# Hashed attention and a gated MLP on one core: weights prepared in DRAM during attention, another order for the first pair, zero matmuls ahead

## The chip, the core and the metric

The kernel runs on one core of a Trainium2 chip. The metric is the device time of one execution in microseconds. A core has five engines that each run their own instructions in program order: TensorE (PE; its weight loads are shown as PEld), VectorE (DVE), ScalarE (ACT), GpSimd (POOL) and SyncE (SP), which here issues nearly all DMAs. Engines wait for each other through semaphores, so a waiting instruction holds up everything behind it on its engine.

## What is computed

Inputs: q, k, v of 4 batches, 8 heads, 768 positions, 64 wide, and the MLP's weights. Everything is float32; the float64 weights w_in and w_out come in as pairs of 32-bit words.

```python
q_bucket = hash of 6 sign bits of q @ proj        # the same for k
scores = where(q_bucket == k_bucket, q @ k.T / 8, -1e9)
attn = softmax(scores);  x = attn @ v             # heads joined: [4, 768, 512]
h = gelu(x @ w_in);  u, v = halves of h           # w_in: [512, 1024]
v_n = layernorm(v) * g_ln
v_s = einsum('ts,bsd->btd', w_sg, v_n) + b_sg     # w_sg: [768, 768]
out = x + (u * v_s) @ w_out                       # w_out: [512, 512]
```

## The kernel before

**Attention** runs over 16 pairs of heads. A pair's q and k come in as one tile each (one buffer: the next pair's load waits until PE has transposed the last one), are transposed on PE (L510), split by ACT and DVE into a high and a low part (L514, L517), and projected for the hash signs (L530, signs on DVE at L533). For each of six query tiles PE forms scores (L550) and DVE takes the row maximum (L555, `mx`); after three of them DVE folds the maxima (L562, `m`) and PE spreads them into a row (L567). Then PE forms the shifted scores of two key tiles at a time (L587, twice 8 matmuls with their halves), ACT takes the exponential (L591, `p`), POOL adds the exponentials up (L604), and after three such groups PE multiplies with v (L616, 24 matmuls). This is called a half here: a pair has two, attention has 32. The sums go to DRAM and back as a reciprocal (L655 to L661), and the half's result xt goes to `xs` in DRAM (L665).

**The MLP** runs over the four batches: `hidden_v` (L780, with gelu and the norm on DVE, ACT and POOL), `hidden_u` (L811), `gate` (L829: all eight PSUM banks are filled tile by tile of w_sg, so that the six tiles are needed one after the other), and `project` (L858).

**Weights.** w_in is taken apart in 16 jobs (`weight_job`, L364 to L388: a load, one POOL multiply, seven DVE steps, one ACT copy), which the planner lets run from the start in DVE's gaps, at the lowest priority. `gate_weights` (L746 to L751) runs after attention: each of the six 128-row tiles of w_sg comes in by four DMAs with pieces of 32 floats (128 bytes), is transposed by DVE, and split by ACT and POOL. `out_weights` takes w_out apart in 16 jobs of half the width (tiles `ow...`, also on L364 to L383) after attention, beside the first gate.

**Order.** The order on each engine is set when the program is built: `Plan` places all steps by costs and priorities (`prio`, two units for a group of attention), with constants such as HID (where `hidden_v` of batch 0 comes in) and WP (priority of the weight jobs). PSUM has eight banks; score tiles take two. In hardware each engine just runs its list.

Of the kernel before, what the change touches and what calls it, by code (L numbers as in the profile page):

```python
# [21 lines left out]
MLP = {"xl": "POOL", "gm": "DVE", "gl": "POOL", "wg": 472.02, "wo": 74.3, "x": 467.58}  # L22
# [3 lines left out]
HID = 275.02  # L26
# [9 lines left out]
class Plan:  # L36
# [76 lines left out]
    def order(self):  # L113
# [13 lines left out]
        free, seq, ready, dma_free, pe, till, lanes = {}, {}, {}, 0.0, {}, {}, []  # L127
# [122 lines left out]
def kernel(  # L250
# [55 lines left out]

    frow = setup.tile([1, 4, P], F32, name="frow")
# [13 lines left out]
    nc.vector.tensor_copy(identr, ident)  # L321
# [9 lines left out]
    msts = [const.tile([P, HT, P], F32R, name=f"m{i}") for i in range(2)]  # L331
    for m in msts:
        nc.vector.memset(m.bitcast(F32), 0.0)
# [8 lines left out]
    wjobs = [(w_in, c, f0, CW, wih, wil, 1.0) for f0 in range(0, FF, CW) for c in range(NC)]  # L342

    def weight_job(plan, tile_of, src, c, f0, CW, th, tl, fac, prio, bank=None, mark=None):
        def part(t):
            return (t() if isinstance(t, Plan.Buf) else t)[:, c, f0:f0 + CW]

        bufs = [(t, (c, f0)) for t in (th, tl) if isinstance(t, Plan.Buf)]
        w = tile_of([P, CW, 2], I32, "w64")
        x, g = tile_of([P, CW], I32, "wx"), tile_of([P, CW], F32, "wg")  # L350
# [570 lines left out]
```

## Time and profile before

| | |
|---|---|
| median of 3 runs | 760.76 us (760.44 to 763.42) |
| the profiled execution, its own time | 760.57 us |
| its span, first to last instruction | 758.7 us |
| PE busy | 731.9 us, 96% of the span |
| DVE / POOL / ACT busy | 557.0 / 466.0 / 375.1 us |
| attention, start to the last product with v | 0 to 446.8 us |
| MLP | 446.8 us to the end |

A busy PE is PE with a matmul in flight. Where PE is busy nearly always, time can only come from its idle stretches, from stretches at the lower clock, and from work that is taken off it. PE's idle before an instruction, with the engine that ended it, is in its timeline and in the list of waits.

### The profile page before, as it was taken

Reading aid. Unit: us, or ns where it says so; the run is one execution under the profiler, and the core shown is the slowest. Engines: PE = TensorE matmul, PEld = TensorE weight load, DVE = VectorE, ACT = ScalarE, POOL = GpSimd, SP = SyncE. Lnnn points to the kernel's source line nnn. Section 1 sums busy time; section 2 is a strip of 40 time slices with the busy share of each in tenths; the row PEclk is TensorE's granted clock in tenths of the full one; section 3 lists DMA queues with packets and bytes.
Section 4 is the critical chain, followed back from the end, with each engine's and each line's share of the span. In section 5 each row is a group of like instructions: output and inputs, shape, how many; then the busy total and the mean of one; then the engine's idle time right before and its main releaser. Section 6 shows DMA issues by size and latency. Waiting matters only on the chain.

```text
span 758.7 us, 14327 instructions
## 1 busy us (share of the span) xinstructions
PE 731.9 (96%) x5348; PEld 594.8 (78%) x5348; DVE 557.0 (73%) x905; ACT 375.1 (49%) x616; POOL 466.0 (61%) x496
## 2 busy tenths in 40 slices
PE   4999999999999999999999999989799999999997
PEld 4686777768787777868686669878798889988996
DVE  6978888988898889887575548669955866447733
ACT  2475565647556664755564456435632236106510
POOL 0478788888868687877767665767753414503230
PEclk9999999999999999999999999999999999999999
DMA  8133444244334423431311125820121552052003
GB/s 184 25 78 78 89 110 118 69 116 123 89 99 106 109 51 96 109 78 50 96 54 33 32 63 111 167 63 21 39 89 56 117 140 69 1 124 44 1 0 111
DMA packets 174597, 60.87 MB, mean 80 GB/s; under 512 B 156736, under 2 KB 167104, under 8 KB 174528
## 3 DMA queue, kind: packets, MB, share of 16 engines
q1 hardware_dynamic: 174080, 59.31, 32.6%
q8 instruction: 42, 0.69, 0.4%
q10 hardware_dynamic: 448, 0.66, 0.3%
q14 instruction: 27, 0.22, 0.1%
HBM read 47.16 MB, written 12.78 MB: 79 GB/s over the span
## 4 chain that ended last, share of the span: by engine, by line
PE 80%; DVE 10%; DMA 5%; issue 2%; ACT 2%; SPq 1%; POOL 0%; DVEq 0%; POOLq 0%; ACTq 0%
PE psb L587 17%; PE psb L616 15%; PE psb L829 11%; PE psb L550 8%; PE psb L858 8%; PE psb L780 6%; PE psb L811 5%; PE psb L530 4%; PE psb L510 3%; PE psb L638 2%; DMA x<-xs 2%; DMA gs<-in_moe_w_sg_dram 1%; DVE mx L555 1%; DMA k<-in_k_dram 1%; PE psb L567 1%
## 5 line engine op out<-in xcount | busy, mean ns | idle before, releaser
L604 POOL TENSOR_TENSOR sum<-sum,p 128x384 f32<-128x384 f32 x256 | 248.8, 1007 | 0.0
L555 DVE TENSOR_REDUCE mx<-psb 128x2 f32<-128x768 f32 x192 | 181.0, 956 | 48.5 <-PE psb L550 41.0
L591 ACT ACTIVATE p<-psb 128x768 f32<-128x768 f32 x192 | 155.3, 814 | 61.5 <-PE psb L587 55.6
L616 PE MATMUL psb<-p,v 128*64 128x385 f32 x768 | 131.2, 491 | 0.0
L604 POOL TENSOR_TENSOR sum<-p,p 128x384 f32<-128x384 f32 x64 | 63.8, 1017 | 73.8 <-ACT p L591 73.8
L616 PEld LDWEIGHTS psb<-p,v 128*64 128x64 f32 x768 | 52.3, 137 | 64.1 <-issue 62.9
L550 PE MATMUL psb<-fk,fq 64*128 64x384 f32 x384 | 68.4, 352 | 1.8 <-DVE fk L533 0.9
L829 PE MATMUL psb<-wgl,zh 128*128 128x384 f32 x192 | 65.4, 340 | 3.7 <-POOL wgl L751 3.7
L587 PE MATMUL psb<-hq,hk 64*128 64x384 f32 x384 | 65.7, 338 | 2.8 <-ACT p L591 1.6
L829 PE MATMUL psb<-wgh,zh 128*128 128x384 f32 x192 | 65.2, 340 | 1.0 <-ACT wgh L750 1.0
L829 PE MATMUL psb<-wgh,zl 128*128 128x384 f32 x192 | 65.1, 339 | 0.0
L587 PE MATMUL psb<-fq,fk 64*128 64x384 f32 x384 | 64.6, 332 | 0.0
L550 PE MATMUL psb<-hk,hq 64*128 64x384 f32 x384 | 64.6, 332 | 0.0
L587 PE MATMUL psb<-lq,hk 64*128 64x384 f32 x384 | 64.5, 332 | 0.0
L587 PE MATMUL psb<-hq,lk 64*128 64x384 f32 x384 | 64.5, 332 | 0.0
L840 POOL TENSOR_TENSOR gs<-gt,gs 128x384 fp32r<-128x384 f32 x32 | 34.1, 1072 | 48.0 <-ACT gs L837 48.0
L858 PE MATMUL psb<-woh,gs 128*128 128x512 f32 x192 | 60.4, 391 | 0.1
L629 ACT COPY un<-psb 128x385 f32<-128x385 f32 x32 | 15.4, 482 | 86.8 <-PE psb L616 86.8
L765 DVE SCALAR_TENSOR_TENSOR h<-h,psb 128x384 f32<-128x384 f32 (+1 forms) x56 | 33.1, 604 | 28.9 <-ACT h L764 28.6
L764 ACT ACTIVATE h<-psb 128x384 f32<-128x384 f32 (+1 forms) x56 | 29.3, 533 | 43.3 <-PE psb L780 39.7
L811 PE MATMUL psb<-xh,wih 128*128 128x384 f32 x128 | 43.6, 341 | 4.1 <-DVE y L769 4.1
L796 POOL TENSOR_TENSOR zl<-y,zh 128x512 fp32r<-128x512 f32 x24 | 32.5, 1353 | 23.6 <-ACT zh L795 23.5
(120 smaller groups left out, 1593.1 us busy)
## 6 DMA issues: line engine op xcount, KB each, us to landing
q<-in_q_dram SPq DMA_DIRECT2D x32, 192.0 KB
k<-in_k_dram SPq DMA_DIRECT2D x32, 192.0 KB
v<-in_v_dram SPq DMA_DIRECT2D x16, 384.0 KB
rs<-r SPq DMA_DIRECT2D x64, 96.0 KB
xs<-xt SPq DMA_DIRECT2D x32, 192.0 KB
x<-xs SPq DMA_DIRECT2D x16, 384.0 KB
rx<-xs SPq DMA_DIRECT2D x96, 64.0 KB
out_dram<-ob SPq DMA_DIRECT2D x24, 256.0 KB
```

The costliest lines, as they stand in the source:

```text
L550: nc.tensor.matmul(sc[kh]()[:, j, :SH], x[0]()[row(j), qs], x[1]()[row(j), kh * SH:(kh + 1) * SH], start=(n == 0), stop=(n == 1))
L555: plan.add(DVE, 0.95, prio, lambda kh=kh: nc.vector.tensor_reduce(mx()[:, i, :, kh], sc[kh]()[:, :, :SH], axis=AX.X, op=ALU.max, negate=Tr ...
L587: nc.tensor.matmul(sc[i]()[:, j, :SH], x()[row(j), ks], y()[row(j), cs], start=(n == 0), stop=(n == 3))
L591: plan.add(ACT, 0.81, prio, lambda i=i: nc.scalar.activation(p[i]()[:, :, :SH], sc[i]()[:, :, :SH], AF.Exp), [sc[i]], [p[i]])
L604: plan.add(POOL, 1.03, prio + 0.6, lambda i=i, j=j, first=first: nc.gpsimd.tensor_add(sums()[:, j], (first or sums)()[:, j, :SH], p[i]()[: ...
L616: nc.tensor.matmul(av()[row(j), :SH + 1], v_()[:, j, kt, :], p[kt]()[:, j, :], start=(kt == 0), stop=(kt == NT - 1))
L765: plan.add(DVE, us + 0.07, prio, lambda: nc.vector.scalar_tensor_tensor(h2()[:, :n], h2()[:, :n], 1.0 / GA, ps()[:, :n], op0=ALU.add, op1= ...
L780: nc.tensor.matmul(ps(), x()[:, ts_], w[:, c, FH:FF], start=(c == 0 and n == 0), stop=(c == NC - 1 and n == 2))
L811: nc.tensor.matmul(ps()[:, :SH], w[:, c, fs], x()[:, cs], start=(c == 0 and n == 0), stop=(c == NC - 1 and n == 2))
L829: nc.tensor.matmul(vp()[:, :SH], z()[:, t, fs], w()[:, t, cs], start=(t == 0 and n == 0), stop=(t == NT - 1 and n == 2))
L840: nc.gpsimd if e == POOL else nc.vector).tensor_sub(gl()[:, cs], gt(), gh()[:, cs].bitcast(F32)),
L858: nc.tensor.matmul(po(), a()[:, ts_], w()[:, f, :], start=(f == 0 and n == 0), stop=(f == NF - 1 and n == 2))
```

## The change

- **Start.** One of the two zeroed tiles `m0` is cleared first; nine matmuls of it with itself (five, then four) are issued ahead of PE's first real work. A few constants move from DVE to POOL (`identr`, half of `pw`). v of the first pair is planned behind its k, g_ln's load behind the first weight job. Weight jobs are planned from the fourth group on, not from the start.
- **w_in** keeps its 16 jobs, each with the same steps, with other priorities (a job every 3.3 groups, then rising).
- **w_out** is taken apart in 8 jobs of full width that follow w_in's in attention. High and low part go to DRAM (`wo_h`, `wo_l`, L382); `out_weights` just loads them (L782).
- **w_sg** is copied DRAM to DRAM in attention, the 128-byte pieces put where the tiles want them (`wgd`, L728, four DMAs in each of pairs 4 to 9); `gate_weights` then loads whole rows (L773). Transposing and splitting stay.
- **Constants** of the planner are other numbers, so the order moves everywhere. EASE is 0, so its branches aren't taken.

```diff
-MLP = {"xl": "POOL", "gm": "DVE", "gl": "POOL", "wg": 472.02, "wo": 74.3, "x": 467.58}
+MLP = {"xl": "POOL", "gm": "DVE", "gl": "POOL", "wg": 463.01, "wo": 6.18, "x": 476.31}
-HID = 275.02
+HID = 282.35
-PREP, SHIFTP, FINP, WSTEP, WP = 5.01, -1.49, 6.21, 37.69, 60
+PREP, SHIFTP, FINP, WSTEP, WP = 4.19, -0.76, 8.79, 37.69, 30
+GPLACE = 4
+EASE = 0
+RATE = 2.45
+WFROM = 7.86
...
+    nc.vector.memset(msts[0].bitcast(F32), 0.0)
...
-    nc.vector.tensor_copy(identr, ident)
+    nc.gpsimd.tensor_copy(identr, ident)
...
+    ojobs = [(w_out, c, f0, CW, None, None, 0.5) for f0 in range(0, DM, CW) for c in range(NF)]
...
+        if th is None:
+            for t, dst, mk in ((hi_, wod[0], wodb[0]), (lo_, wod[1], wodb[1])):
+                plan.add("SP", 0.57, prio, lambda t=t, dst=dst: nc.sync.dma_start(dst[:, c, f0:f0 + CW], t().bitcast(F32)),
+                         wh if t is hi_ else wl, [(mk, (c, f0))], dma=0.4)
...
+    for i in range(5):
+        nc.tensor.matmul(psb[:, 6, :P], msts[0][:, 0].bitcast(F32), msts[0][:, 0].bitcast(F32), start=True, stop=True)
     for i in range(4):
         nc.tensor.transpose(psb[:, 7, i:i + 1], frow[:, i, :], ident[:1, :1])
     nc.vector.tensor_copy(fcol, psb[:, 7, 0:4])
+    for i in range(4):
+        nc.tensor.matmul(psb[:, 6, :P], msts[0][:, 0].bitcast(F32), msts[0][:, 0].bitcast(F32), start=True, stop=True)
...
-        for i, job in enumerate(wjobs):
-            weight_job(plan, w_tile, *job, WSTEP * i + WP, BANKED and ps_one or None, win)
...
+                if c == 1 and GPLACE <= n < GPLACE + NT:
+                    t = n - GPLACE
+                    for h in range(P // Q):
+                        c0 = t * P + h * Q
+                        dma(2 * g + 20, 0.6, lambda eng, t=t, h=h, c0=c0: eng.dma_start(
+                            wgd[t][h * Q:(h + 1) * Q].rearrange("b (f a) -> b f a", a=Q),
+                            w_sg[:, c0:c0 + Q].rearrange("(f b) a -> b f a", b=Q)), [ticks[-1]], [(wgdb, (t, h))])
+                while conv and WFROM + RATE * conv[0][0] <= 2 * g:
+                    at_, job, args = conv.pop(0)
+                    job(plan, w_tile, *args, 2 * g + WP, after=[ticks[-1]])
...
     def gate_weights(prio):
-            for g in range(P // Q):
-                c0 = t * P + g * Q
-                dma(prio + t - 5, 0.6, lambda eng, w=w, g=g, c0=c0: eng.dma_start(
-                    w()[g * Q:(g + 1) * Q].rearrange("b (f a) -> b f a", a=Q),
-                    w_sg[:, c0:c0 + Q].rearrange("(f b) a -> b f a", b=Q)), w=[(w, g)], e=WSG)
+            dma(prio + t - 5, 1.1, lambda eng, w=w, t=t: eng.dma_start(w(), wgd[t]), [wgdb], [w])
...
     def out_weights(prio):
-        CO = 128
-        for f0 in range(0, DM, CO):
-            for c in range(NF):
-                weight_job(plan, lambda sh, dt, tag: tile_of(sh, dt, "o" + tag, 1), w_out, c, f0, CO, woh, wol, 0.5, prio)
+        for c in range(NF):
+            for i, w in enumerate((woh, wol)):
+                dma(prio + c, 0.75, lambda eng, i=i, w=w, c=c: eng.dma_start(w()[:, c, :].bitcast(F32), wod[i][:, c, :]), [wodb[i]], [(w, c)])
```

Three places show what the planner makes of it. The first is DVE at the start, from the first pair's low part of k (lk) to the second pair's. `wy`, `wx`, `wil` are steps of a weight job, `fq` and `fk` the signs, `mx` the maxima. Before:

```order
L517 SCALAR_TENSOR_TENSOR lk_0_279<-psb,hk_0_274 128x768
L373 TENSOR_SCALAR wy_283<-w_0_247 128x256
L533 TENSOR_SCALAR fq_0_291<-psb,fcol 128x768
L374 SCALAR_TENSOR_TENSOR wx_293<-w_0_247,wy_283 128x256
L375 SCALAR_TENSOR_TENSOR wx_293<-wg_281,wx_293 128x256
L377 TENSOR_SCALAR wy_283<-wx_293 128x256
L533 TENSOR_SCALAR fk_0_303<-psb,fcol 128x768
L378 SCALAR_TENSOR_TENSOR wy_283<-w_0_247,wy_283 128x256
L386 TENSOR_TENSOR wx_293<-wx_293,wy_283 128x256
L517 SCALAR_TENSOR_TENSOR lq_0_317<-psb,hq_0_310 128x768
L555 TENSOR_REDUCE mx_93<-psb 128x2 x6
```

The same stretch of DVE now:

```order
L520 SCALAR_TENSOR_TENSOR lk_0_284<-psb,hk_0_282 128x768
L541 TENSOR_SCALAR fq_0_286<-psb,fcol 128x768
L541 TENSOR_SCALAR fk_0_306<-psb,fcol 128x768
L520 SCALAR_TENSOR_TENSOR lq_0_310<-psb,hq_0_300 128x768
L568 TENSOR_REDUCE mx_96<-psb 128x2 x6
L575 TENSOR_REDUCE m_71<-mx_96 128x6
```

The weight steps are gone from there. The second place is DVE in one late half of attention (between the 24th and the 25th `m`). Before:

```order
L663 SCALAR_TENSOR_TENSOR xt_4049<-un_3614,rs_3972 128x384
L533 TENSOR_SCALAR fq_6_4061<-psb,fcol 128x768
L533 TENSOR_SCALAR fk_6_4083<-psb,fcol 128x768
L657 RECIPROCAL sq_4023<-sq_4023 128x6
L373 TENSOR_SCALAR wy_4088<-w_15_3933 128x256
L374 SCALAR_TENSOR_TENSOR wx_4091<-w_15_3933,wy_4088 128x256
L375 SCALAR_TENSOR_TENSOR wx_4091<-wg_3989,wx_4091 128x256
L377 TENSOR_SCALAR wy_4088<-wx_4091 128x256
L378 SCALAR_TENSOR_TENSOR wy_4088<-w_15_3933,wy_4088 128x256
L555 TENSOR_REDUCE mx_93<-psb 128x2 x6
```

The same half of DVE now:

```order
L541 TENSOR_SCALAR fq_6_4089<-psb,fcol 128x768
L673 RECIPROCAL sq_4053<-sq_4053 128x6
L541 TENSOR_SCALAR fk_6_4114<-psb,fcol 128x768
L377 TENSOR_TENSOR wx_3961<-wx_3961,wy_3955 128x256
L371 TENSOR_SCALAR wy_4122<-w_15_4036 128x256
L379 SCALAR_TENSOR_TENSOR wil<-wx_3961,wih 128x256
L372 SCALAR_TENSOR_TENSOR wx_4131<-w_15_4036,wy_4122 128x256
L568 TENSOR_REDUCE mx_96<-psb 128x2
L373 SCALAR_TENSOR_TENSOR wx_4131<-wg_4137,wx_4131 128x256
L375 TENSOR_SCALAR wy_4122<-wx_4131 128x256
L376 SCALAR_TENSOR_TENSOR wy_4122<-w_15_4036,wy_4122 128x256
L377 TENSOR_TENSOR wx_4131<-wx_4131,wy_4122 128x256
```

Five weight steps have become eight; before, the jobs end with the half after this, now they go on to the end of attention. The third place is SP behind attention's last sums (`r`, `rs`), where the tiles `gs` of w_sg are loaded. Before:

```order
L746 DMA gs_5637<-in_moe_w_sg_dram 32x24x32 x4
L665 DMA xs_111<-xt_5680 128x384
L665 DMA xs_111<-xt_5698 128x384
L746 DMA gs_5732<-in_moe_w_sg_dram 32x24x32 x2
L364 DMA ow_0_5749<-in_moe_w_out_dram 128x256
L851 DMA rx_5757<-xs_108 32x16x32 x4
L851 DMA rx_5785<-xs_108 32x16x32 x4
L727 DMA x_5820<-xs_109 128x768
L746 DMA gs_5732<-in_moe_w_sg_dram 32x24x32
```

SP at the same place now:

```order
L773 DMA gs_5774<-wgd 128x768
L677 DMA rs_5788<-r_0_236 64x384 x2
L677 DMA rs_5817<-r_1_238 64x384 x2
L773 DMA gs_5833<-wgd 128x768
L773 DMA gs_5864<-wgd 128x768
L681 DMA xs_111<-xt_5880 128x384
L681 DMA xs_111<-xt_5902 128x384
L773 DMA gs_5923<-wgd 128x768
L782 DMA woh_5952<-wo_h 128x512
```

Tiles four to six now stand ahead of the loads for `project` (rx), with one DMA each.

## Rows read from the trace of the kernel before

**Rows 1.** The page: busy time in us (share of the 758.7) and instructions by engine

```profile
PE 731.9 (96%) x5348; PEld 594.8 (78%) x5348; DVE 557.0 (73%) x905; ACT 375.1 (49%) x616; POOL 466.0 (61%) x496
```

**Rows 2.** PE's timeline, MLP: start, us, line, out<-in, [idle before <-who ended it]

```profile
488.94 0.44 PE L829 MATMUL psb<-wgl,zh 128*128 128x384 f32 x1 [1.46 <-POOL wgl L751]
494.22 0.44 PE L829 MATMUL psb<-wgh,zh 128*128 128x384 f32 x1 [0.99 <-ACT wgh L750]
496.87 0.69 PE L829 MATMUL psb<-wgl,zh 128*128 128x384 f32 x1 [2.21 <-POOL wgl L751]
...
537.58 0.45 PE L811 MATMUL psb<-xh,wih 128*128 128x384 f32 x1 [1.55 <-DVE y L769]
542.52 0.45 PE L811 MATMUL psb<-xh,wih 128*128 128x384 f32 x1 [2.55 <-DVE y L769]
```

**Rows 3.** PE's timeline at the start of the kernel

```profile
4.58 1.51 PE L510 MATMUL psb<-ident,q 128*128 128x128 f32 x6 [2.16 <-DMA q<-in_q_dram]
8.62 1.51 PE L510 MATMUL psb<-ident,k 128*128 128x128 f32 x6 [2.52 <-DMA k<-in_k_dram]
...
10.88 0.52 PE L530 MATMUL psb<-hq,pwh 128*128 128x384 f32 x1
...
12.48 0.33 PE L530 MATMUL psb<-hk,pwl 128*128 128x384 f32 x1
...
14.62 0.85 PE L510 MATMUL psb<-ident,q 128*128 128x128 f32 x6 [1.63 <-DMA q<-in_q_dram]
16.31 0.44 PE L550 MATMUL psb<-fk,fq 64*128 64x384 f32 x2 [0.85 <-DVE fk L533]
```

**Rows 4.** The chain that ended last, its pieces up to 40 us: start, us, what

```profile
14.08 0.34 DVE wx L374
...
25.73 0.43 DVE wx L374
26.16 1.00 DVE fk L533
```

**Rows 5.** SP's timeline at the start: the first pair's q and v, and the next q

```profile
0.74 1.02 SPq L493 DMA_DIRECT2D q<-in_q_dram  x2
...
2.98 4.81 SPq L499 DMA_DIRECT2D v<-in_v_dram  x2
...
9.26 0.95 SPq L493 DMA_DIRECT2D q<-in_q_dram  x2
```

**Rows 6.** PE's timeline in attention: two products with v

```profile
204.67 4.10 PE L616 MATMUL psb<-p,v 128*64 128x385 f32 x24
...
230.80 4.10 PE L616 MATMUL psb<-p,v 128*64 128x385 f32 x24
```

**Rows 7.** Busy time by window, engines in turn; then PEclk, DMA share, GB/s

```profile
45.00:337.00 292.00, 290.35 (x2631) 217.84 (x2632) 255.18 (x340) 172.84 (x263) 233.56 (x241) 1.00 0.38 95
...
494.00:500.00 6.00, 3.57 (x11) 3.32 (x12) 2.86 (x6) 1.61 (x4) 4.25 (x5) 0.72 0.57 122
...
542.50:550.00 7.50, 7.48 (x34) 7.49 (x35) 7.08 (x16) 6.12 (x14) 6.28 (x6) 0.77 0.20 56
```

**Rows 8.** Groups by line, DVE, 45 to 337 us: count | busy, mean ns | idle

```profile
L386 DVE TENSOR_TENSOR wx<-wx,wy 128x256 f32<-128x256 f32 x14 | 11.4, 811 | 0.3
...
L373 DVE TENSOR_SCALAR wy<-w 128x256 int32<-128x256 int32 x13 | 9.4, 726 | 1.6 <-DMA w<-in_moe_w_in_dram 1.5
```

**Rows 9.** DVE's timeline: one weight step beside POOL's sums

```profile
113.36 1.11 DVE L374 SCALAR_TENSOR_TENSOR wx<-w,wy 128x256 int32<-128x256 int32 x1
```

**Rows 10.** DVE's timeline in the MLP: a tile of w_sg, and its wait

```profile
485.08 0.98 DVE L749 STREAM_TRANSPOSE gs<-gs 128x768 f32<-128x768 f32 x1 [2.85 <-DMA gs<-in_moe_w_sg_dram]
```

**Rows 11.** Busy time by window (last half of attention; hidden_v), DVE alone, then PEclk, DMA share, GB/s

```profile
412.46:428.61 16.15, 7.84 (x12) 1.00 0.12 38
...
520.00:545.00 25.00, 23.89 (x56) 0.98 0.09 28
```

**Rows 12.** PE's waits in the whole span: total us, times, longest us

```profile
PE psb L587 <- ACT p L591: 1.6, 4, 0.5
```

More of the change, by code (lines that the diff above doesn't have):

```diff
@@ L330 @@
         nc.vector.memset(t[:, :, :, 2:3], EMPTY)
[L331 to L333 removed]
+    nc.vector.memset(msts[1].bitcast(F32), 0.0)
     fcol = const.tile([P, 4], F32, name="fcol")
@@ L366, in vec @@
         def vec(fn, r, wr, fast=False):
-            plan.add("DVE", 0.16 + CW / (1920.0 if fast and port else 960.0), prio, fn, r, wr, port=port)
-        lo, hi, xf, zi = (lambda: w()[:, :, 0]), (lambda: w()[:, :, 1]), (lambda: x().bitcast(F32)), (lambda: zf().bitcast(I32))
-        plan.add("SP", 0.55, prio - 2, load, [], [w], dma=0.73 * CW / 256)
+            plan.add("DVE", 0.14 + CW / (1920.0 if fast else 960.0), prio, fn, r, wr, port=True)
+        lo, hi, xf, yf, xi = (lambda: w()[:, :, 0]), (lambda: w()[:, :, 1]), (lambda: x().bitcast(F32)), (lambda: y().bitcast(F32)), x
@@ L395 @@
     win = plan.buf("win", 1)
+    wod = [dram.tile([P, NF, DM], F32, name=f"wo_{i}") for i in "hl"]
+    wgd, wgdb = dram.tile([NT, P, S], F32, name="wgd"), plan.buf("wgdb", 1)
+    wodb = [plan.buf(f"wodb{i}", 1) for i in range(2)]
     xd = [[plan.buf(f"xd_{b}_{c}", 1) for c in range(NC)] for b in range(B)]
@@ L521, in parts @@
             plan.add(ACT, 0.81, prio, high, [tp], [hh])
-            plan.add(DVE, 0.95, prio, low, [tp, hh], [lo])
+            if 1 <= st.n <= EASE:
+                ft = st.ft[s]
+                plan.add(ACT, 0.81, prio, lambda: nc.scalar.mul(two(ft).bitcast(F32), tp()[:, :, :SH], fac), [tp], [ft])
+                plan.add(POOL, 1.88, prio, lambda: nc.gpsimd.tensor_sub(lo(), ft().bitcast(F32), hh().bitcast(F32)), [ft, hh], [lo])
+            else:
+                plan.add(DVE, 0.95, prio, low, [tp, hh], [lo])
         def features(st, s, prio):
@@ L536, in features @@
             plan.add(PE, 1.044, prio, project, [hh, lo, ft], [fp])
-            plan.add(DVE, 1.07, prio, sign, [fp], [ft])
+            if 1 <= st.n <= EASE:
+                plan.add(ACT, 0.81, prio, lambda: nc.scalar.copy(two(ft).bitcast(F32), fp()[:, :, :SH]), [fp], [ft])
+                plan.add(POOL, 1.88, prio, lambda: nc.gpsimd.tensor_scalar(
+                    ft(), ft().bitcast(F32), fcol[:, 2 * s:2 * s + 1], fcol[:, 2 * s + 1:2 * s + 2], op0=ALU.is_gt, op1=ALU.mult), [ft], [ft])
+            else:
+                plan.add(DVE, 1.07, prio, sign, [fp], [ft])
         def largest(st, t, prio):
```

64 lines of the change are left out of this document (31 added, 33 removed).

## The prediction, made before the kernel was run

> **What bounds the kernel now.** I read the page's busy times first: PE is busy for 731.9 of 758.7 us [rows 1], so only its 26.8 us of idle time, and stretches at a lower granted clock, are to be had. PE's timeline then says where these are. At the start it waits 2.16 us for q, 2.52 for the first k, 1.63 for the second q and 0.85 for `fk` [rows 3]; smaller waits lie between. In the MLP five waits make 8.8 us: 1.46 + 0.99 + 2.21 = 4.66 for tiles of w_sg inside the first gate, and 1.55 + 2.55 = 4.10 for DVE's `y` in `hidden_v` of batch 1 [rows 2]. In attention PE hardly waits: four waits for ACT, 1.6 us together, are the largest item [rows 12].
>
> The windows add the clock [rows 7]. From 45 to 337 us it is granted in full. From 494 to 500 us the mean is 0.72 and from 542.5 to 550 us 0.77: each time PE had just stood idle, and part of the window ran at the lower of the two levels (1.2 instead of 2.4 GHz). At the start the same shows in single matmuls: 0.52 us, later 0.33 [rows 3], after PE had waited for loads.
>
> The profiled execution took 760.57 us, 1.87 more than its span and 0.2 under the median; the sum is made against 760.57.
>
> **The start.** Before, v (two transfers, 768 KB) is issued ahead of everything but q and k, taking SP until 7.8 us, and the next q follows only at 9.26 [rows 5]. Now v stands behind the next q. Three things follow.
>
> (a) k shares the queues with less. q, issued at 0.74, was there at 4.58, so a k without v beside it should be ready when PE has transposed q, at about 6.1: up to 2.5 us earlier than 8.62 [rows 3, 5]. (b) The next q's transposes (0.85 us, up to 1.5 at the low clock [rows 3]) now stand on PE ahead of k's projections, not behind them. That load can be issued when PE has read the old tile, at about 6; issuing takes 0.95 [rows 5], and landing took 2.8 us for the first q (1.76 to 4.58) and 4.4 for the second (10.21 to 14.62): it arrives at 9.8 to 11.4. With its transposes, k's six projections (1.1 us, 1.9 at the low clock) and `fk` (1.0 [rows 4]), `fk` is done at 12.7 to 15.8. Before, it was done just ahead of 16.31, where the scores begin [rows 3]: 0.5 to 3.5 us are won. (c) The chain that ended last runs through eight weight steps on DVE, the first at 14.08 us, the last at 25.73 ahead of the second pair's `fk`, 2.97 us in all [rows 4]. Three lie ahead of the first `fk`, in (b)'s stretch; the other five, 1.8 us, behind it. The second order piece shows them gone.
>
> Together 2.3 to 5.3, with 3.8 in the middle. The nine zero matmuls lie inside the wait that ends at 4.58: nine of 0.25 us (1.51 / 6 [rows 3]) are 2.3 us, and about 4 us pass there nearly without work on PE, so they cost nothing if `m0` is cleared in time. What they can bring is the clock: six projections at 0.32 us apart, where later ones are 0.17 apart [rows 3], are 0.9 us, most of it beside waits for loads; I count 0.2. The start is worth **−4.0**. If the next q lands late, PE stands there with k's projections behind it, and the first `fk` gains nothing; with half of the later steps covered by something else, −1.0 is the other bound.
>
> **The MLP's first gate.** All eight banks are filled tile by tile, so a late tile stops PE. Tiles come in by pieces of 128 bytes; DVE waited 2.85 us for one [rows 10]. Now whole rows are read and, as the third order piece shows, all six tiles stand ahead of rx. The 4.66 us go, and with them the slow stretch: 6 us at 0.72 are 1.7 us too much, 1.4 after what idle time of it has been counted. The pieces of 128 bytes now move in pairs 4 to 9, where the queues are 0.38 busy [rows 7] and nobody waits for the result; hidden. What is late next is a tile's transpose (0.98 us on DVE [rows 10]) and split on ACT and POOL, which now have all of `hidden_v` of batch 0 ahead of them.
>
> **The MLP's `hidden_v`.** From 520 to 545 us DVE is busy 23.89 of 25 us [rows 11], so DVE is the bound there. Of the 56 steps there 21 belong to w_out; at the mean of 23.89 / 56 = 0.43 us they are 9 us. With w_out ready in DRAM they go, DVE needs 15 of the 25 us, and 4.10 + 7.5 × 0.23 = 4.10 + 1.7 us [rows 2, 7] go too. The eight loads of w_out, 256 KB each, have the whole first gate to land.
>
> Sum of the MLP: −(4.66 + 1.4 + 4.10 + 1.7) = **−11.9**. The other bound is one of the two places keeping its stall: −5.8.
>
> **Attention pays.** Eight more jobs put 56 steps on DVE, 8 on POOL and 8 on ACT, and 24 placements, 16 stores and 8 loads on SP, whose stores wait for ACT and DVE with the next q and k queued behind; q and k have a whole pair's time, so that is hidden. DVE is the question. Two products with v of the same half lie 230.80 − 204.67 = 26.13 us apart, a half is 13.07 [rows 6]. From 45 to 337 us DVE is busy 255.2 us [rows 7], of which 97 weight steps in seven groups (the first and the last are shown [rows 8]) have 72.1 us, 0.743 each. The other 183.1 us over 22.3 halves are 8.2 us a half. 13.07 − 8.2 leaves room for 6.5 steps.
>
> Counted between the `m` of the order now, halves 4 to 20 hold 3 to 6 steps, as before. From the 21st on the counts are 8, 6, 7, 5, 8, 7, 6, 3, 7, 6, 7 and 11 in the last. A half of 8 needs 14.14 us, 1.07 too much: 2.1 for two. A half of 7 is 0.33 over, 1.3 for four, hidden if the maxima run ahead as in the halves with room. The last half took 16.15 us from `m` to `m`, since `hidden_v` already runs in it, and DVE was busy for 7.84 of them [rows 11]; with 11 steps (8.2) and two more of `hidden_v` (1.4, by what its steps take in the MLP) it needs 17.4, 1.3 too much. Between 2.1 and 4.7 I take **+3.5**. Bounds: 0, if `m` has slack everywhere; +10, if a step in the twelve full halves costs 0.85, near the 0.81 group [rows 8] (8.2 + 6.75 × 0.85 = 13.94, 0.87 over, 10.4 for twelve). The waits for ACT [rows 12] stay.
>
> Sum: 760.57 − 4.0 − 11.9 + 3.5 = **748.2 us**.
>
> **Rivals.** *DVE's steps beside POOL (slower).* A weight step next to POOL's sums took 1.11 us [rows 9], half as much again as the mean. If the twelve full halves run at that, each needs 8.2 + 6.75 × 1.11 = 15.7 and is 2.6 us too long: +31, and 760.57 − 15.9 + 31 = **776**. It is as slow as before from 15.9 = 12 × (8.2 + 6.75 s − 13.07), s = 0.92 us per step. For it: the 1.11; against it: 97 steps at a mean of 0.743 in a stretch in which POOL was busy 80% of the time [rows 7]. On this mechanism the Trainium skill ("SBUF — State Buffer", section "SBUF: two separate sides") has a rule that DVE and GpSimd share a port pair as a lock held for a whole instruction. By it alone a step that meets one of POOL's sums waits for its end, as the 1.11 us suggest [rows 9], and the time would be this rival's; by the mean of 0.743 most steps meet none, or POOL waits instead.
>
> *One stall stays.* Clearing the gate's loads or DVE shows the next late thing in the same place, about half of the 11.9: **754**. For it: five waits on three engines in one stretch [rows 2]; against: both causes are removed, not moved.
>
> *The start doesn't gain.* The next q's load is late, −1.0 instead of −4.0: **751**.
>
> *Only moved.* w_out's steps cost in attention what they cost in the MLP: +10 instead of +3.5, **755**; with one of the MLP's stalls left as well it is 760, no change.
>
> **How the numbers follow.** Forecast with its own range 743 to 751: 0.58. One stall left 0.13, no gain at the start 0.10, only moved 0.10, slower by DVE 0.09. A measurement of this kernel can tell about 0.5%, 3.8 us: faster is under 757.0, slower over 764.4. Faster: 0.58 + 0.13 + 0.10 + 0.04 of the moved ones (755 to 760) = 0.85; same: 0.06 of these and 0.02 of the slower case, 0.08; slower 0.07. The range reaches from all bounds at their best, 760.57 − 5.3 − 11.9 = 743.4, with the clock's 0.9 us 742, to 757, which takes in one stall or moved work.
>
> **What will show it.** Right: the scores begin at 11 to 14 us instead of 16.31, no PE wait of over 0.5 us for `wgh`, `wgl` or `y` in the MLP, a full granted clock there, 13.1 to 14.2 us between products with v late in attention, and PE idle of 10 to 13 us in all. Wrong: PE waiting for `m` or for the maxima in the halves from 21 on (DVE), weight steps over 0.9 us there, PE waiting for the second q at the start, or a tile of w_sg or w_out that arrives late because its placement did.

## The result, and the profile after

The changed kernel takes 749.21 us (median of 4 runs, 747.89 to 750.39) against 761.81 us before (4 runs, 760.44 to 763.42): the ratio is 0.983, with a 95% interval of 0.980 to 0.986. The profiled execution took 750.39 us, the slowest of its four, with a span of 748.6; all that follows is read from it and set against the 758.7 us of span before. So between the two profiles the change is 10.1 us, and between the medians 12.6.

The page of the changed kernel: span, then PE's busy time (share of span) and instructions. PE is busy 734.2 us, 2.3 more than before [rows 1], while the span is 10.1 shorter.

```profile
span 748.6 us, 14297 instructions
PE 734.2 (98%) x5366; PEld 593.1 (79%) x5366; DVE 564.2 (75%) x876; ACT 368.9 (49%) x592; POOL 452.8 (60%) x461
```

Busy share says little of where the 10.1 us come from. The starts of the 32 products with v on PE's timeline cut the span in stages (us from the span's start):

| | 1st product | 30th product | last product | end of span |
|---|---|---|---|---|
| before | 33.66 | 413.71 | 442.75 | 758.7 |
| after | 29.91 | 415.98 | 449.19 | 748.6 |

So the start won 3.75 us, the 29 halves behind it lost 6.02 (386.07 instead of 380.05), and from the last product on 16.54 are won. In the last pair 12 more matmuls of `hidden_v` (0.23 us each) now stand between the 30th and the 31st product, 24 where 12 were. Those 2.8 us only changed sides of the cut: of the 4.17 us lost between the 30th and the last product 1.4 are a loss, and the MLP won 13.7.

**The MLP** has lost its waits and its slow stretches. These are the windows of [rows 7] again in the changed kernel: busy time of PE, PEld, DVE, ACT and POOL, then PEclk, DMA share, GB/s.

```profile
494.00:500.00 6.00, 6.00 (x37) 5.97 (x35) 2.75 (x5) 2.41 (x4) 4.63 (x4) 1.00 0.91 205
542.50:550.00 7.50, 7.50 (x44) 7.50 (x43) 6.31 (x13) 6.22 (x12) 3.22 (x4) 1.00 0.00 1
```

Both are full and at the full clock, and no wait of PE of 0.15 us or more is left behind the last product; in [rows 2] there were five.

**The start**, PE's timeline of the changed kernel (start, us, operation, idle before):

```profile
1.32 2.50 PE L427 MATMUL psb<-m 128*128 128x128 f32 x10 [1.32 <-DVE m L311]
3.61 1.91 PE L432 MATMUL psb<-m 128*128 128x128 f32 x8
5.46 0.40 PE L429 MATMUL psb<-ident,frow 1*128 1x1 f32 x4
5.79 0.87 PE L513 MATMUL psb<-ident,q 128*128 128x128 f32 x6
6.50 0.82 PE L513 MATMUL psb<-ident,k 128*128 128x128 f32 x6
...
10.99 0.85 PE L513 MATMUL psb<-ident,q 128*128 128x128 f32 x6 [1.38 <-DMA q<-in_q_dram]
...
14.07 0.45 PE L563 MATMUL psb<-fk,fq 64*128 64x384 f32 x2 [1.17 <-DVE fk L541]
```

k no longer waits (2.52 us in [rows 3]), and the scores begin at 14.07 instead of 16.31. But the nine zero matmuls are 18 instructions on PE, not nine: PE is at them until about 5.46, and q's transposes, at 4.58 before, begin at 5.79.

**Attention** lost 6.0 us without showing them as idle: the waits of 0.15 us or more between the 1st and the 30th product sum to 2.5 us (1.55 before). Late in attention PE is busy 122.19 of 123 us, before 123.00, and yet does less. The window from 280 to 403 us, before and then after, engines as above:

```profile
280.00:403.00 123.00, 123.00 (x1118) 92.76 (x1116) 95.14 (x126) 71.58 (x108) 94.41 (x100) 1.00 0.31 78
```

```profile
280.00:403.00 123.00, 122.19 (x1080) 89.38 (x1077) 111.63 (x158) 71.52 (x111) 95.06 (x101) 1.00 0.38 98
```

DVE has 16.5 us more to do there and is busy 91% of the time. What PE pays is seen in one half, the one from 307.87 to 322.40 (14.53 us, the same half 13.49 before). First DVE, then PE, in the middle of it:

```profile
313.02 0.96 DVE L568 TENSOR_REDUCE mx<-psb 128x2 f32<-128x768 f32 x1 [1.16 <-PE psb L563]
...
315.02 0.42 DVE L373 SCALAR_TENSOR_TENSOR wx<-wg,wx 128x256 f32<-128x256 f32 x1
315.48 0.29 DVE L375 TENSOR_SCALAR wy<-wx 128x256 int32<-128x256 int32 x1
315.80 1.24 DVE L376 SCALAR_TENSOR_TENSOR wy<-w,wy 128x256 f32<-128x256 uint32 x1
316.96 3.54 DVE L568 TENSOR_REDUCE mx<-psb 128x2 f32<-128x768 f32 x4
```

```profile
316.61 0.34 PE L602 MATMUL psb<-fq,fk 64*128 64x384 f32 x2
316.90 0.44 PE L563 MATMUL psb<-fk,fq 64*128 64x384 f32 x2
317.18 0.34 PE L563 MATMUL psb<-hk,hq 64*128 64x384 f32 x2
317.97 0.45 PE L602 MATMUL psb<-hq,hk 64*128 64x384 f32 x2 [0.45 <-DVE mx L568]
```

Three weight steps stand between two maxima, and PE waits for the banks that the maxima hold. Only 0.45 us of it are listed as idle. The matmul at 316.90 starts 0.29 behind the one ahead of it and lasts 0.44 instead of 0.33, and the next starts 0.28 behind it; the distance is 0.17 elsewhere. So some 0.2 us are lost there that count as busy. This half has five matmuls of scores or projections with such a long head (over 0.42 us), the same half before has two. Over the eleven halves from the 19th to the 30th product there are 36 of them, before 16, and these halves lost 5.05 us, of which 0.8 are listed as idle: about 0.2 us for each head more. So here the distance between products must be read, not the idle column. And the half isn't full: ahead of the maximum at 313.02 DVE stands idle for 1.16 us, waiting for PE.

### The profile page after: what moved, and what is told of

Its sections match the earlier page's. It is cut to its first block, busy times and chain, and to the rows that moved or that the text cites. A ratio compares the mean times of both kernels' runs of the same rounds, so it can differ in the third digit from the quotient of the medians.

```text
span 748.6 us, 14297 instructions
## 1 busy us (share of the span) xinstructions
PE 734.2 (98%) x5366; PEld 593.1 (79%) x5366; DVE 564.2 (75%) x876; ACT 368.9 (49%) x592; POOL 452.8 (60%) x461
## 4 chain that ended last, share of the span: by engine, by line
PE 91%; DVE 5%; DMA 2%; issue 1%; ACT 1%; SPq 0%; DVEq 0%; ACTq 0%
PE psb L602 16%; PE psb L632 16%; PE psb L853 13%; PE psb L835 9%; PE psb L563 9%; PE psb L882 9%; PE psb L804 9%; PE psb L538 5%; PE psb L513 3%; DVE mx L568 2%; PE psb L654 2%; PE psb L580 1%; DVE wy L376 1%; DMA w<-in_moe_w_in_dram 1%; DVE wy L375 1%
## 5 line engine op out<-in xcount | busy, mean ns | idle before, releaser
L568 DVE TENSOR_REDUCE mx<-psb 128x2 f32<-128x768 f32 x192 | 178.3, 954 | 26.7 <-PE psb L563 22.2
L620 POOL TENSOR_TENSOR sum<-p,p 128x384 f32<-128x384 f32 x64 | 65.3, 1041 | 84.8 <-ACT p L607 84.7
L563 PE MATMUL psb<-fk,fq 64*128 64x384 f32 x384 | 70.7, 362 | 2.9 <-DVE mx L568 1.6
L814 POOL TENSOR_TENSOR mv<-mv,epsr 128x1 f32<-128x1 f32 x24 | 13.8, 576 | 90.2 <-DVE mv L813 90.2
L856 DVE TENSOR_TENSOR gt<-psb,b_bc 128x384 f32<-128x384 f32 x32 | 17.7, 555 | 49.7 <-PE psb L853 45.9
L563 PEld LDWEIGHTS psb<-fk,fq 64*128 64x128 f32 x384 | 36.3, 184 | 18.6 <-issue 5.6
```

Of the source, the lines that this page charges most:

```text
L563: nc.tensor.matmul(sc[kh]()[:, j, :SH], x[0]()[row(j), qs], x[1]()[row(j), kh * SH:(kh + 1) * SH], start=(n == 0), stop=(n == 1))
L568: plan.add(DVE, 0.95, prio, lambda kh=kh: nc.vector.tensor_reduce(mx()[:, i, :, kh], sc[kh]()[:, :, :SH], axis=AX.X, op=ALU.max, negate=Tr ...
L620: plan.add(POOL, 1.03, prio + 0.6, lambda i=i, j=j, first=first: nc.gpsimd.tensor_add(sums()[:, j], (first or sums)()[:, j, :SH], p[i]()[: ...
```

## The experiments

All change the changed kernel. The stages of each run, as above. The twelve matmuls of `hidden_v` (2.8 us) that changed sides stand ahead of the last product in the changed kernel, in the run with w_sg gathered, with the jobs begun 3 groups earlier, with no or six zero matmuls and with the jobs spread; in the other five they stand behind it, as before, so the column of the last product is 2.8 us lower there.

| run | median, us (runs) | 1st product | 30th | last | span |
|---|---|---|---|---|---|
| changed kernel | 749.21 (4) | 29.91 | 415.98 | 449.19 | 748.6 |
| no w_out steps on DVE | 745.78 (4) | 29.51 | 413.61 | 441.50 | 744.5 |
| w_out in the MLP | 760.40 (10) | 29.73 | 414.18 | 443.24 | 759.1 |
| w_sg gathered in the MLP | 759.86 (10) | 30.06 | 417.35 | 450.40 | 758.7 |
| weight jobs early | 755.81 (7) | 29.04 | 422.16 | 451.24 | 754.0 |
| jobs begun 3 groups earlier | 748.86 (4) | 29.32 | 415.45 | 446.77 | 746.7 |
| no zero matmuls | 746.17 (1) | 28.94 | 413.28 | 445.04 | 744.4 |
| the same, pw on DVE | 750.61 (1) | 30.99 | 415.70 | 447.47 | 748.8 |
| six zero matmuls, pw on DVE | 746.11 (1) | 29.26 | 413.23 | 444.99 | 744.3 |
| the same, timed | 747.33 (5) | 29.44 | 413.55 | 445.35 | 745.7 |
| ... and two buffers for w | 749.68 (4) | 29.46 | 411.62 | 440.70 | 748.0 |
| ... or two for wx and wy | 746.83 (4) | 28.79 | 413.44 | 442.56 | 745.1 |
| ... and two for w, jobs spread | 745.47 (4) | 28.89 | 412.27 | 443.78 | 743.7 |

### Does DVE's work on w_out cost attention its time?

```diff
 def weight_job(plan, tile_of, src, c, f0, CW, th, tl, fac, mark, prio, after=()):
+    if th is None:
+        # load, POOL's multiply into g, one ACT copy into y, stores of y and g
+        return
```

> The changed kernel with the seven DVE steps of each of w_out's eight jobs left out: the load, POOL's multiply, one ACT copy and the two stores to DRAM stay, so that what is stored for w_out is not its value. Measure: from the 19th to the 30th product with v the kernel before took 143.3 us, the changed one 148.4. Theory (DVE's steps between the maxima cost it): the halves in which only w_out's steps ran, the 25th to the 30th, get back to 13.07 (1.8 us), the last half loses its wait for ACT's exponentials (1.4): some 146.5 us for the stretch, 2 to 4 us less in all, 745 to 747. Rival (stores, loads, POOL or the queues cost it): 148 us and 749.

It took 745.78 us, ratio to before 0.980 (0.978 to 0.983), some 3.4 us under the changed kernel. From the 24th to the 30th product it needs 78.44 us, before 78.50, the changed kernel 80.34: the 1.8 us came back as expected. The whole stretch from the 19th product is 147.4, not 146.5, because the five halves from the 19th to the 24th product stay long: 68.97 us, 68.03 in the changed kernel, 64.84 before. There all steps are w_in's, 8, 6, 7, 5 and 8 a half, where before there were 4 or 5. So of attention's 6.0 us 1.8 come from DVE's steps of w_out, which this run shows, and 3.2 lie where only w_in's jobs run, which the new priorities push together; that these jobs are the cause is argued from the place here.

### Could w_out stay in the MLP?

```diff
-    ... (weight_job, 2.7, [w + (None,) for w in ojobs])
-            dma(prio + c, 0.75, lambda eng, ...: eng.dma_start(w()[:, c, :].bitcast(F32), wod[i][:, c, :]), ...)
+            # 16 jobs of 128 columns in out_weights: five DVE steps, three of POOL, two of ACT each
```

> The changed kernel with w_out converted in the MLP beside the first gate, as before (16 jobs of half width, five DVE steps each), w_sg still placed in attention. Theory: attention as in the run without w_out's steps (146.5 us from the 19th to the 30th product), and hidden_v of batch 1 short of DVE again, 4.1 + 1.7 us and some small waits: 749.2 - 3 + 6.3 = 752.5. Rival (the gate's late tiles were the whole stall, and the order now leaves DVE room in the MLP): 746.

With it the planner's constant `wo`, the place of `out_weights`, is back at 74.3. It took 760.40 us, ratio 1.000 (0.998 to 1.002): 8 us more than expected, and against both theories. Attention did as expected (146.9 us). The MLP cost 13.6 us more (315.86 from the last product, with 2.8 us of matmuls on this side, against 299.41), as long as before (315.95). PE's timeline there:

```profile
534.79 0.44 PE L859 MATMUL psb<-xh,wih 128*128 128x384 f32 x1 [2.92 <-DVE y L817]
570.67 0.50 PE L906 MATMUL psb<-woh,gs 128*128 128x512 f32 x1 [2.83 <-DVE y L817]
575.64 0.50 PE L906 MATMUL psb<-woh,gs 128*128 128x512 f32 x1 [1.64 <-ACT woh L804]
576.61 0.80 PE L906 MATMUL psb<-wol,gs 128*128 128x512 f32 x1 [0.47 <-POOL wol L805]
```

The first wait is of the kind in [rows 2]; the others are new. DVE's steps of w_out by tile (min/median/max ns, first and last start), and one place on DVE's timeline, say why:

```profile
L797 DVE TENSOR_SCALAR owy<-ow x16: 219/228/970, 474.0 to 572.6; 128x128 int32<-128x128 int32 x16
```

```profile
530.09 0.23 DVE L797 TENSOR_SCALAR owy<-ow 128x128 int32<-128x128 int32 x1 [1.44 <-DMA ow<-in_moe_w_out_dram]
```

The sixteen jobs share one buffer and so form one chain, with loads that DVE waits for in between (11.3 us in seven waits) and `y` behind them. Its first steps run from 476.3 to 570.2 us before, when the gate waits for its tiles, and from 474.0 to 572.6 here, where the gate waits for none: it is no faster. `project` of batch 0, which needs its results, begins at 564 us (577 before) and still waits for them at 575. In the changed kernel w_out is there early, and `project` begins at 503. So the conversion, not the gate's tiles, set the end of this stretch: taking away the tiles' stall alone only moved the wait to the chain's end. w_out's move is worth 13.6 us in the MLP on top of w_sg's, not the 5.8 that I had counted.

### Could w_sg be gathered by the gate itself?

```diff
-                if c == 1 and GPLACE <= n < GPLACE + NT: ... # four placements
-            dma(prio + t - 5, 1.1, lambda eng, w=w, t=t: eng.dma_start(w(), wgd[t]), [wgdb], [w])
+            for g in range(P // Q): ... # four gathers of 32x24x32 from w_sg
```

> The changed kernel with w_sg gathered in pieces of 128 bytes by gate_weights, as before, and no placement in attention; w_out still by way of DRAM. Theory: attention unchanged, 148.4 us from the 19th to the 30th product; the first gate waits for tiles again, 4.66 + 1.4 us: 755. Rival (the placements slow attention's own transfers or engines): up to 3 us back in attention, 752.

It took 759.86 us, ratio 0.999 (0.997 to 1.001), 4.9 us above the first theory. The stretch named there is unchanged (148.1 us), but the placements aren't in it: in the changed kernel they are issued from 129.8 to 266 us, ahead of the 19th product. The stretch around them, from the 9th to the 20th product, takes 145.3 us without them and 144.5 to 146.5 in the nine runs that have them and the same pace of weight jobs. So the placements cost nothing that these runs can tell, and the second theory falls. From the last product on it takes 308.3 us, 8.9 more. PE's waits, and the window around them:

```profile
500.39 0.44 PE L850 MATMUL psb<-wgh,zh 128*128 128x384 f32 x1 [4.05 <-ACT wgh L772]
502.28 0.69 PE L850 MATMUL psb<-wgl,zh 128*128 128x384 f32 x1 [1.45 <-POOL wgl L773]
```

```profile
500.00:506.00 6.00, 4.16 (x13) 3.91 (x14) 0.74 (x1) 0.34 (x1) 1.81 (x1) 0.63 0.99 199
506.00:510.00 4.00, 4.00 (x18) 4.00 (x17) 0.34 (x2) 2.30 (x3) 2.81 (x2) 0.70 0.10 39
```

5.5 us of waiting, and behind it a stretch at the lower level (0.63 and 0.70 granted over 10 us), which makes most of the other 3.4. (The span is 1.2 us longer by attention too: in the half after the third product DVE waits 3.25 us for a load of w, PE 1.86 in turn, and the granted clock is at the lower level for 3.4 us behind it.)

With either part undone the kernel is no faster than before, with both in place it is 12.6 us faster: whichever cause is left in the MLP keeps most of the time that both took there, while attention pays for w_in's crowd in each case.

### Does the loss follow the steps?

```diff
-PREP, SHIFTP, FINP, WSTEP, WP = 4.19, -0.76, 8.79, 37.69, 30
+PREP, SHIFTP, FINP, WSTEP, WP = 4.19, -0.76, 8.79, 37.69, 8
-WFROM = 7.86
+WFROM = 2
```

> The changed kernel with the weight jobs earlier (first at the 3rd half, less delay): 6 to 8 steps a half from about the 10th half to the 29th, none in the last three. Theory: the loss goes where the steps are: halves 10 to 18 take 13.3 to 13.6 us instead of 13.07, the stretch from the 19th to the 30th product stays near 147 to 148, the last two halves lose 1 to 2 us less; in all 748 to 751. Rival (something of the late halves themselves, such as hidden_v's loads or SP's queue): halves 10 to 18 stay at 13.07 and the late ones stay long.

From the 9th to the 18th product it follows them: the changed kernel takes 119.5 us there with 43 steps, here it is 123.5 with 62, some 0.2 us for each step more. The last two halves are back to 16.80 and 12.28 us (19.48 and 13.73, of which 2.8 are the matmuls that changed sides). But the late stretch got longer still, 150.2 us (147 to 148 expected), with 59 steps where the changed kernel has 70; PE waits there three times for ACT's exponentials, 1.4 us, which it didn't in the changed kernel. The whole took 755.81, beyond what I had named. So the loss comes with the crowd, but the number of steps in a half doesn't give it, and that the late halves have a cost of their own isn't excluded.

Then the start alone is moved, the delay kept:

```diff
-WFROM = 7.86
+WFROM = 2
```

> The changed kernel with its weight jobs begun 3 groups earlier and nothing else: the halves hold 4 to 6 steps up to the 15th, then 4, 7, 6, 8, 3, 4, 7, 6, 7, 8, 5, 5, 6, 5, 7, 6, 9. Theory (each step beyond 6 in a half costs 0.3 to 1 us): the stretch from the 19th to the 30th product, 148.4 us in the changed kernel, takes 146.5 to 147.5, the last two halves 1 us less, in all 747 to 748. Rival (it is DVE's mean load that costs, not its peaks): 749.

748.86 us: not to be told from the changed kernel. The stretch came down to 147.1 as expected, but the two halves to the 18th product took 28.0 instead of 26.3, and the 10th half 14.95, where PE waited 1.75 us for ACT's exponentials. The peak was moved, not removed; this run doesn't settle whether peaks or DVE's mean load cost more.

### The start: what do the zero matmuls do?

```diff
-    for i in range(5):
-        nc.tensor.matmul(psb[:, 6, :P], msts[0][:, 0].bitcast(F32), ...)
...
-    for i in range(4):
-        nc.tensor.matmul(psb[:, 6, :P], msts[0][:, 0].bitcast(F32), ...)
```

> The changed kernel without the nine zero matmuls ahead. In the changed kernel they ran from 1.32 to 5.46 us, past the time at which q was there in the kernel before (4.58), and the first product with v began at 29.91 us. Theory (they hold PE up longer than the clock gives back): q's transposes at 4.6 us at the low clock, the next q issued and landed about 1 us earlier, scores at 13.1 instead of 14.07, first product at 29.0 to 29.4. Rival (they earn their place by the clock): transposes and projections at the low clock, scores at 14.5 or later, first product at 30.5.

```diff
-                (nc.vector if s else nc.gpsimd).tensor_scalar_mul(pv[...], ...)
+                nc.vector.tensor_scalar_mul(pv[...], ...)
```

> The changed kernel without the nine zero matmuls and with all of pw on DVE, as before, so that the copy of pw on ACT waits for one engine and its table load need not wait (it ran at 2.60 before, at 5.20 in the changed kernel). Theory (the load of the next q sets the first fk, not hq): as without the zero matmuls alone, first product within 0.2 us of that run. Rival (ACT's table load is on the path once the matmuls are gone): hq 0.7 us earlier and the first product 0.5 to 0.7 us earlier than in that run.

> The changed kernel with six zero matmuls instead of nine (12 passes of 0.23 us, from 1.32 to about 4.1) and all of pw on DVE. Theory: PE is free when q lands and the clock stays up: q's transposes at 4.6 us, scores at 13.0, first product at 28.8 to 29.1, the best of the starts. Rival (q's landing varies more than this gains): 29.5 to 30.

The first has the first product at 28.94 us, the second at 30.99, with the same matmuls on PE in the same order. PE's timelines, first without the zero matmuls, then with pw on DVE as well:

```profile
9.52 0.51 PE L534 MATMUL psb<-hq,pwl 128*128 128x384 f32 x1
9.84 0.36 PE L534 MATMUL psb<-lq,pwh 128*128 128x384 f32 x1
10.04 0.82 PE L509 MATMUL psb<-ident,q 128*128 128x128 f32 x6
...
13.07 0.44 PE L559 MATMUL psb<-fk,fq 64*128 64x384 f32 x2 [1.17 <-DVE fk L537]
```

```profile
9.57 0.52 PE L534 MATMUL psb<-lq,pwh 128*128 128x384 f32 x1
10.53 1.51 PE L509 MATMUL psb<-ident,q 128*128 128x128 f32 x6 [0.44 <-DMA q<-in_q_dram]
...
12.80 0.52 PE L534 MATMUL psb<-hk,pwh 128*128 128x384 f32 x1
...
15.13 0.45 PE L559 MATMUL psb<-fk,fq 64*128 64x384 f32 x2 [1.17 <-DVE fk L537]
```

In the first the matmuls come at the fast pace from about 9.84 us on, in the second every projection up to the first scores is still at the slow one (0.52 us). The trace's record of the granted clock begins just there, at 9.88 and at 14.19 us, with the full clock. The 0.27 us by which pw's new place brings `hq` forward (6.59 instead of 6.86) don't matter against this. The first did what its theory said (scores at 13.07), and its rival falls; of the second neither theory had it: without zero matmuls the start depends on when the clock rises, and that differed by over 4 us between two nearly equal programs.

With six the first product came at 29.26, 29.44, 29.46, 28.79 and 28.89 us in five runs (the last three with other buffers), with nine at 29.04 to 30.06 in six runs: 0.4 us earlier on average, with pw on DVE changed as well. But not for the reason in the theory. With nine the record of the clock begins at 4.25 to 6.66 us, with six at 4.92 to 10.56, so six don't hold the clock up; in the run of 29.26 it begins at 10.56, and the scores at 13.40 instead of 13.0. What is gained is that PE is free when q lands (transposes at 4.7 to 5.0 us instead of 5.2 to 6.0), and what a late rise costs is small as long as it comes ahead of k's projections, as in all but the one at 30.99. None at all can gain 1 us or lose 1. The times of these three, one run each, can't tell 1 us.

### Three kernels built on this

> The kernel with six zero matmuls and all of pw on DVE again, timed. Theory: its profile's first product was 0.65 us earlier than the changed kernel's and its last product did not wait for ACT (1.4 us, which came and went between runs of the same order): 747 to 748.5, 0.5 to 2 us under the changed kernel's 749.2. Rival (the single look of 746.1 holds): 746.

747.33 us, ratio 0.981 (0.979 to 0.984): as the theory had it. The single run of 746.11 lies within the spread of these five (745.01 to 748.08).

```diff
 def w_tile(shape, dt, tag):
-    return early.ring(shape, dt, tag)
+    return early.ring(shape, dt, tag, 2 if tag in ("w64",) else 1)
```

> The same with two buffers instead of one for a weight job's loaded piece (w). In the changed kernel DVE waited 2.33 us near 59 us for such a load with the maxima behind it, and PE 0.93 in turn; in the run with w_sg gathered it was 3.25 and 1.86. Theory (the load can now run ahead): no wait of DVE for w of over 0.3 us, the fourth half at 12.6 instead of 13.0 to 16.4 us, some 1 to 2 us less: 745.5 to 746.5. Rival (the waits were in slack but for the first): as without it.

The wait that it was to remove, in the changed kernel; first DVE, then PE:

```profile
58.52 0.52 DVE L379 SCALAR_TENSOR_TENSOR wil<-wx,wih 128x256 fp32r<-128x256 f32 x1 [0.48 <-ACT wih L378]
61.37 0.30 DVE L371 TENSOR_SCALAR wy<-w 128x256 int32<-128x256 int32 x1 [2.33 <-DMA w<-in_moe_w_in_dram]
61.58 2.68 DVE L568 TENSOR_REDUCE mx<-psb 128x2 f32<-128x768 f32 x3
```

```profile
62.59 0.44 PE L563 MATMUL psb<-fk,fq 64*128 64x384 f32 x2 [0.93 <-DVE mx L568]
```

It is gone: DVE waits for no w, the fourth half took 12.61 us, and the 29 halves 382.2 us, 2 less than with one buffer. Yet the kernel took 749.68 us, ratio 0.986 (0.983 to 0.988), against the theory. The planner now puts the loads of rx, 16 in all, ahead of w_sg's last two tiles on SP, and PE waits in the first gate, with the granted clock at the lower level for 3.4 us behind the first wait. SP's timeline, then PE's:

```profile
475.49 8.37 SPq L875 DMA_DIRECT2D rx<-xs  x8
483.91 0.49 SPq L773 DMA_DIRECT2D gs<-wgd  x1
...
485.43 5.85 SPq L875 DMA_DIRECT2D rx<-xs  x8
491.33 0.49 SPq L773 DMA_DIRECT2D gs<-wgd  x1
```

```profile
491.42 0.53 PE L853 MATMUL psb<-wgl,zh 128*128 128x384 f32 x1 [1.45 <-POOL wgl L776]
498.63 0.45 PE L853 MATMUL psb<-wgl,zh 128*128 128x384 f32 x1 [1.22 <-POOL wgl L776]
```

Instead of w, the tiles that are stored from:

```diff
-    return early.ring(shape, dt, tag)
+    return early.ring(shape, dt, tag, 2 if tag in ("wx", "wy") else 1)
```

> Instead, two buffers for wx and wy, from which w_out's parts are stored. In the changed kernel DVE waited 1.49 us near 441 for a store to have read wy, the last exponentials waited on ACT behind the step after it, and PE's last product 1.37. Theory (the stores hold the next job's first step): no such wait, the last halves shorter by up to 1.4 us and the halves from the 25th on by 0.2 each: 745.5 to 747. Rival (with the steps crowded there anyway another takes its place): as without it.

746.83 us, ratio 0.982 (0.980 to 0.985): within the theory, and within 0.5 us of the kernel with one buffer. The halves from the 24th to the 30th product got nothing (80.44 us, 80.20 with one buffer). The last product waits for nothing in either, so the wait of 1.4 us in the changed kernel isn't shown to be cured by the buffers. What the runs do show: six have the same order of DVE in the last pair, and in the two in which DVE waits there for a store of wy (1.49 us in the changed kernel, 1.33 with w_sg gathered) PE's last product waits (1.37 and 1.20); in the four others (no zero matmuls, the same with pw on DVE, six in two runs) neither wait is there.

The last has two buffers for w and another pace:

```diff
-RATE = 2.45
-WFROM = 7.86
+RATE = 2.6
+WFROM = 2
```

> Two buffers for w, six zero matmuls, pw on DVE, and the weight jobs begun earlier and a little further apart: halves of 3 to 6 steps up to the 18th, then 6, 7, 5, 4, 5, 6, 8, 6, 7, 3, 5, 6, 5, 10 and 14 after the last maximum. Theory (peaks cost): the stretch from the 19th to the 30th product at 146 to 147 instead of 148.4 us and no wait for w: 744.5 to 745.5, the fastest. Rival (steps pushed behind the last maximum delay hidden_v): 746 or more, PE waiting for y.

745.47 us, ratio to before 0.980 (0.977 to 0.983), the lowest median of all. The stretch from the 19th to the 30th product took 146.5 us, and PE waits nowhere in the MLP for over 0.3 us. Its interval overlaps the changed kernel's (0.980 to 0.986), which was timed beside other runs; that it is faster is likely (3.7 us between the medians, 2.5 by the ratios), not proven.

## Why the prediction was right, and where it was not

The forecast was 748.2 us in a range of 742 to 757; 749.21 was measured. The direction and the range held, and so did the mechanisms of the start and of the MLP. That the number came out within 1 us is in part luck. Two of the three terms were too small, one on each side: attention by 3.9 us, the MLP by 1.8. What is left, 2.2 us with the start, stands between the forecast and the profiled execution (750.39); that is the slowest of the four, and the median came out nearer.

Of the signs named ahead, the MLP's came, without a wait and at the full clock. The scores began at 14.07 us, just behind the 11 to 14; PE's idle, taken as there from span and busy time, is 14.4 us and not 10 to 13; the late halves take 12.8 to 14.5 us, not 13.1 to 14.2. Two signs of being wrong showed as well, in small: PE waited 1.38 us for the second q, which the sum had allowed for, and for maxima in the late halves, which is the term that came out too small.

**The start**, −4.0 forecast, −3.75 measured. The steps held: k was ready when q had been transposed; the next q's transposes stood on PE ahead of k's projections and waited for their load (1.38 us); the first `fk` ended in time for scores at 14.07, in the stretch from 12.7 to 15.8 us that I had worked out. From the first scores to the first product it took 15.84 us instead of 17.35, 1.5 won where 1.8 was counted. Wrong was the step on the zero matmuls: "nine of 0.25 us are 2.3 us". A call gives two instructions on PE here (the timeline has x10 and x8), so they were 4.1 us and ended 0.9 us behind the 4.58 at which q had been there before. I had the unit price from transposes, one instruction each, and did not ask how many instructions one call makes.

**The MLP**, −11.9 forecast, −13.7 measured. Both stalls went, and their slow stretches with them. Where the other 1.8 us lie isn't measured in full: long heads that count as busy around the listed waits, as in attention, are a part, and I had summed listed waits only. The run with w_out in the MLP shows that this term was also reasoned too simply: I treated w_out's move as relief for DVE in `hidden_v`, and it was also the end of a chain of almost 100 us that `project` waits for.

**Attention**, +3.5 forecast within 0 and +10, +7.4 measured (6.0 over 29 halves, 1.4 at the last product). The mechanism was named, the size was wrong, and the step that failed is the model: room of 13.07 − 8.2 us a half, filled by steps of 0.743. The steps took less than that, not more. In the window from 280 to 403 us 55 of them took 37.1 us, 0.675 each; these are the first and the last of their eight groups by line (count, busy us, mean ns, idle before):

```profile
L372 DVE SCALAR_TENSOR_TENSOR wx<-w,wy 128x256 int32<-128x256 int32 x8 | 7.5, 940 | 1.1 <-DMA wo_l<-wx 1.0
...
L379 DVE SCALAR_TENSOR_TENSOR wx<-wx,wy 128x256 fp32r<-128x256 f32 x4 | 2.1, 523 | 0.5 <-ACT wy L378 0.5
```

And DVE was idle 11.4 us of those 123, at least 0.3 us in every half from the 19th product to the 30th and 1.5 in the one shown above. So it isn't that the half was too full: runs of two or three steps stand between maxima that PE waits for, and DVE is idle at other places of the same half. A sum of durations against the room in a half came out too low here, since it leaves out where the steps stand.

With this the slow rival falls too. It needed steps of 0.92 us on average, and they took 0.675. Of the three steps above one took 1.24 us and another 0.42; the slow one, from 315.80, ran beside a sum of POOL, the other beside none:

```profile
315.75 2.16 POOL L620 TENSOR_TENSOR sum<-p,p 128x384 f32<-128x384 f32 x2 [2.59 <-ACT p L607]
```

With these single steps the Trainium skill's rule of the port pair ("SBUF — State Buffer", section "SBUF: two separate sides") agrees; it sets the price of some steps, not of the mean.

The 1.4 us at the last product are a wait that I had priced at nothing: w_out's parts are stored from `wy` and `wx`, each with one buffer, so the next job's first step must wait until a store has read it. (In the runs with the same order the two waits came and went together, as told above; that the store's wait alone makes PE's isn't proven, since three of the steps behind it also took 1.1 us each here, and 0.3, 0.4 and 1.1 with six zero matmuls.) DVE, then ACT, then PE in the changed kernel:

```profile
441.37 0.29 DVE L371 TENSOR_SCALAR wy<-w 128x256 int32<-128x256 int32 x1 [1.49 <-DMA wo_h<-wy]
```

```profile
446.61 0.42 ACT L378 ACTIVATE wy<-wx 128x256 fp32r<-128x256 f32 x1 [3.38 <-DVE wx L377]
446.94 2.20 ACT L607 ACTIVATE p<-psb 128x768 f32<-128x768 f32 x3
```

```profile
449.19 4.10 PE L632 MATMUL psb<-p,v 128*64 128x385 f32 x24 [1.37 <-ACT p L607]
```

ACT's part of the same job stands ahead of the last three exponentials, and with it PE's last product. I had looked at the stores from SP's side alone.

The placements of w_sg were rightly counted at nothing: without them the halves around their places are no shorter. Of the waits for ACT in attention, which were to stay, one of 0.62 us was left (1.6 in [rows 12]). What would have made the prediction wrong, a late tile of w_sg, did come up, though only in the kernel with two buffers for w, and there behind the loads of rx.

Left open: what decides when PE's clock rises at the start (9.88 us in one run and 14.19 in a nearly equal program, 4.25 to 6.66 in the six with the same nine matmuls ahead), and what share of attention's loss is DVE's order and what its mean load. No kernel with the same steps in better places inside a half was made.

## What to carry to other kernels

Where one engine is busy 98% of the time, measure the distance between its milestones and don't sum its idle column: waits of some 0.2 us at the head of a matmul counted as busy here, and cost 0.2 to 1 us in a half of 13. Moving work into gaps of an engine that also feeds the bound one can cost more than the gaps' sum says, since a step that isn't urgent delays the urgent one behind it; and a load or a store that such a step waits for is waited for by all that stands behind. Judge parts of a change that remove stalls of the same stage together: here undoing either one gave back the whole gain.

## What the hardware showed that I had not expected

- A float32 matmul of 128 by 128 with itself (the zero matmuls) is two instructions of 0.23 us at the slow pace, where a transpose of the same size by the identity is one of 0.25.
- At the start the PEclk column of the windows reads 1.00 (as from 10 to 11.5 us before) while projections come 0.32 us apart instead of 0.17. In the MLP the same pace goes with 0.50 granted (496.8 to 499.6 us before). The column says nothing there: the trace's record of the granted clock begins only at 11.60 us before, at 5.48 in the changed kernel and at 9.88 and 14.19 without zero matmuls, each time with the full clock and where the matmuls become fast. So up to there the slow level is read from the matmuls' distances.
- ACT's table load (1.28 us) ran at 2.60 us before and at 5.20 in the changed kernel: pw is written by two engines there, and the table load ahead of the copy of pw now waits for DVE's part (5.20 <-DVE pw). With pw on DVE alone and no zero matmuls it ran at 1.98.
